# Attention scores in three float32r passes over high and low parts, and a new table of places for the attention steps

## The chip, the cores and the metric

The kernel runs on one core of one Trainium2 chip, in one launch. The metric is the device time in microseconds (us) of that launch. Engines are named as in the profile: PE is TensorE's matrix multiply, PEld its weight loads, DVE is VectorE, ACT is ScalarE, POOL is GpSimd, SP is SyncE, which here issues most DMAs.

## The reference

Three stages follow one another, all in float32:

```python
# 1. attention, batch 4, heads 8, sequence 576, head_dim 64
scores = q @ k.T / sqrt(64)
scores = where(scores >= max(scores) - tau, scores, -1e9)      # tau = 0.02
attn   = exp(scores - max(scores)); attn = attn / (sum(attn) + 1e-9)
out    = attn @ v                                              # -> x: 2304 rows of 512
# 2. mixture of experts, 8 experts, 512 -> 1024 -> 512, one expert per row
#    (argmax of the cosine of row and expert embedding)
# 3. the same again, the expert chosen by argmax(x @ w_gate)
```

The thresholding makes the scores' precision matter: which keys stay depends on differences of 0.02 and less.

## The kernel before, in words

**Attention** (class Attn, lines 127 to 500) takes the 32 heads as 16 pairs. For each pair: q and k of two heads are loaded by SP with the rows on the partitions (`load`); PE transposes them into a PSUM tile of the pool S (`transpose`, L226 to L231, steps `tk` and `tq`); ACT copies q out (L236, step `cpq`) and DVE copies k out (L237, step `cpk`). Then head A lies on partitions 0 to 63 and head B on 64 to 127 of the tiles Tq and Tk. The 576 queries of both heads make nine score tiles r of 128 queries x 576 keys (tile 8 holds the last 64 queries of both heads). Five steps `scores t` compute them (L240 to L249): for t < 4 the tiles 2t and 2t+1, one of each head, as matmuls of 64 rows by 288 keys that alternate between the heads, and for t = 4 tile 8 as matmuls of all 128 rows. All matmuls of attention are float32; the trace has two records, each with its own weight load, for one float32 matmul. So a step `scores t` is 8 records (t < 4) or 4 (t = 4).

Each score tile then goes `least` (DVE, L256: scaled copy out of PSUM and row minimum of the negated scores), `bound` (POOL, L263: threshold), and one of two ways to the unnormalised probabilities p. The first is `exp all` (ACT, L288), then `mask` (DVE, L293: compare with the threshold, multiply, row sum). The second is `beyond` (DVE, L268: a large number where the score is out), `add` (POOL, L272), `exp` (ACT, L283 with the row sum). `MASK_FIRST` (L137) lists the tiles that go the second way: 2, 4 and 6 in pairs 1 to 13, none in pair 0 and in the last two. After that PE transposes p in 128x128 blocks (L312, L310, steps `t A0` to `t R4`), ACT copies the blocks out (L322), PE multiplies by v (`av`, L338 and L334), ACT copies the result (L344), PE transposes it back and adds the router's logits (`out rows`, L354), DVE normalises (L362 to L367), SP stores. After every fourth pair the rows' places among the experts are worked out (`route`, on PE, DVE and POOL; `route slots` is 3.2 us of DVE in one step).

**The order** on each engine is fixed when the program is built. `ops` (L382 to L459) lists every step with its engine, an assumed duration, what it depends on and which buffers it takes and frees; `schedule` (L75) plays this list through, on each engine always the ready step with the lowest number `PERIOD * pair + PRIO[kind]`, and the steps are emitted in the order of their starts. `PERIOD` is 17.0 (L52) and `PRIO` a table by hand (L55 to L65). Buffers (L458): S, the PSUM tiles of transposed q, k and of scores, has two, so that a step `scores t` with t < 4 needs both; raw q and k, Tq and Tk two each, sn (scores out of PSUM) five, b three, p fourteen, raw v three.

**The expert layers** (class Moe) run afterwards; they already split every float32 operand into a high float32r part (ACT copy, L779) and a low one (DVE subtraction from PSUM, L782) and take three passes, high x high, high x low, low x high (L790, L801).

Of the kernel before, what the change touches and what calls it, by code (L numbers as in the profile page):

```python
# [22 lines left out]
B, H, S, D = 4, 8, 576, 64  # L23
# [25 lines left out]
BIG = 1e30  # L49
PAIRS = B * H // 2  # L50

PERIOD = 17.0  # L52


PRIO = {'first': -93.7, 'warm': -10000, 'emb norm': 10.0, 'emb t': 11.0, 'emb put': 12.0, 'params': 0.0, 'sign': 20.0, 'weights': 0.0,  # L55
        'ldk': -24.0, 'ldq': -24.0, 'ldv': -14.0, 'tk': -7.0, 'tq': -6.5, 'cpk': -6.5, 'cpq': -6.0,
        **{f'scores {t}': 3.2 * t for t in range(5)}, **{f'bound {t}': 3.2 * t + 2 for t in range(5)},
        **{f'least {r}': 1.6 * r + .5 for r in range(9)}, **{f'exp all {r}': 1.6 * r + 1.2 for r in range(9)}, **{f'mask {r}': 1.6 * r + 2 for r in range(9)},
        **{f'beyond {r}': 1.6 * r + 1 for r in range(9)}, **{f'add {r}': 1.6 * r + 1.5 for r in range(9)}, **{f'exp {r}': 1.6 * r + 3 for r in range(9)},
        'inverse': 17.0, **{f't {h}{k}': 16.0 + 2.6 * k + (h == 'B') for h in 'AB' for k in range(5)}, **{f'copy {h}{k}': 16.5 + 2.6 * k + (h == 'B') for h in 'AB' for k in range(5)},  # L60
        't R0': 29.5, 't R4': 30.0, 'copy R0': 30.0, 'copy R4': 30.5, **{f'av {k}': 18.0 + 2.6 * k for k in range(5)}, 'av R': 32.0,
        'out copy M': 30.0, 'out copy R': 32.5, 'out rows 0': 31.0, 'out rows 1': 32.0, 'out rows R': 33.0, 'out scale 0': 31.5, 'out scale 1': 32.5, 'out scale R': 33.5,
        'logits': 34.0, 'route argmax': 36.0, 'route prefix': 37.0, 'route count': 38.0, 'route slots': 38.0, 'route perm': 39.0, 'route add': 40.0,
        'plans': 20.0, 'choose count': 41.0, 'choose': 41.5,
        'w1 hi': 100.0, 'w1 lo': 101.0, 'ld w1': 102.0}  # L65


class Op:
# [4 lines left out]


def schedule(ops, caps, verbose=False):  # L75


# [49 lines left out]
class Attn:  # L127
# [6 lines left out]

    UNITS = [(h, k) for k in range(5) for h in 'AB'] + [('R', 0), ('R', 4)]

    MASK_FIRST = (), (2, 4, 6), ()  # L137
    DVE_COPY = (), (), ()

    def __init__(s, nc, tc, early, late, ident, q, k, v, tau, emb, xd, lg, moe):  # L140
# [89 lines left out]
        for t in range(4): nc.tensor.transpose(ps[:, 128 * t:128 * t + 128], raw[:, 128 * t:128 * t + 128], s.id)  # L230
        nc.tensor.transpose(ps[:, 512:512 + n], raw[0:n, 512:640], s.id[0:n, 0:n])  # L231

    def copy(s, j, nm):
        st = s.pair[j]
        st['T' + nm] = s.qk.tile([128, 640 if nm == 'q' else 576], F32, tag='T' + nm, name='T' + nm)
        if nm == 'q': s.nc.scalar.activation(out=st['Tq'], in_=st['psq'], func=AF.Copy)  # L236
        else: s.nc.vector.tensor_copy(st['Tk'], st['psk'])  # L237


    def scores(s, j, t):  # L240
        nc, st = s.nc, s.pair[j]
        q, k = st['Tq'], st['Tk']
        rr = (2 * t, 2 * t + 1) if t < 4 else (8,)
        for r in rr: st['ps', r] = s.psS.tile([128, 1024], F32, tag='S', name='psS')
        for i in range(2):
            ks = slice(i * 288, i * 288 + 288)
            for h, r in enumerate(rr):
                p = slice(64 * h, 64 * h + 64) if t < 4 else slice(0, 128)
                nc.tensor.matmul(st['ps', r][:, (224, 512)[i]:(512, 800)[i]], q[p, 128 * t:128 * t + 128], k[p, ks], start=True, stop=True)  # L249

    def least(s, j, r):

# [129 lines left out]
    def ops(s, params, done, prio=None):  # L382
# [13 lines left out]
        for j in range(PAIRS):  # L396
            ld, put = {}, {}
            for nm in 'kqv':
                if j == 0 and nm in 'kq': ld[nm] = op('ld' + nm, j, 'X', 0, lambda: None, alloc=['raw' + nm], lat=4.2 if nm == 'k' else 6.2)
                else: ld[nm] = op('ld' + nm, j, 'SP', 1.95 if nm == 'q' else 1.3, lambda j=j, nm=nm: s.load(j, nm), [first], alloc=['raw' + nm], lat=3.0)  # L400
            for nm in 'kq':
                step = lambda m, j=j, nm=nm: lambda: m(j, nm)
                x = op('t' + nm, j, 'P', .55, step(s.transpose), [ld[nm]], alloc=['S', 'T' + nm], free=['raw' + nm])
                if nm == 'k': put[nm] = op('cpk', j, 'D', .70, step(s.copy), [x], free=['S'])
                else: put[nm] = op('cpq', j, 'A', .60, step(s.copy), [x], free=['S'])
            if j == 0: emb.deps.append(put['k'])

            if j == 2:
                x = op('params', j, 'SP', 2.6, params, [last], lat=2.5)
                op('sign', j, 'D', .2, s.moe.sign, [x])  # L410
            if 1 <= j < 15: op('plans', j, 'G', 1.2, lambda j=j: s.moe.plans(j - 1), [last])

            P = {}
            for t in range(5):
                rr = (2 * t, 2 * t + 1) if t < 4 else (8,)
                last = op(f'scores {t}', j, 'P', 1.0, lambda j=j, t=t: s.scores(j, t), list(put.values()) + [last], t, alloc=['S'] * len(rr), free=[] if t < 4 else ['Tq', 'Tk'])
                least = [op(f'least {r}', j, 'D', .76, lambda j=j, r=r: s.least(j, r), [last], r, alloc=['sn'], free=['S']) for r in rr]
                th = op(f'bound {t}', j, 'G', .25, lambda j=j, t=t: s.bound(j, t), least, t)
                for r, l in zip(rr, least):
                    step = lambda m, r=r, j=j: lambda: m(j, r)  # L420
                    e = [emb_put] if j == 0 else []
                    if r not in s.of_pair(s.MASK_FIRST, j):
                        x = op(f'exp all {r}', j, 'A', .70, step(s.exp_all), [l], r, alloc=['b'])
                        P[r] = op(f'mask {r}', j, 'D', .80, step(s.mask), [x, th] + e, r, alloc=['P'], free=['sn', 'b'])
                    else:
                        x = op(f'beyond {r}', j, 'D', .50, step(s.beyond), [th], r, alloc=['b'])
                        x = op(f'add {r}', j, 'G', 1.36, step(s.add), [x], r, free=['sn'])
                        P[r] = op(f'exp {r}', j, 'A', .80, step(s.exp), [x] + e, r, alloc=['P'], free=['b'])
            inv = op('inverse', j, 'D', .5, lambda j=j: s.inverse(j), list(P.values()))

            U, AV, X = {}, None, []
            for u in s.UNITS:
                h, k = u
                n = f'{h}{k}'
                step = lambda m, a=u, j=j: lambda: m(j, a)
                rr = {'A': range(0, 8, 2), 'B': range(1, 8, 2), 'R': [8]}[h]
                small = u == ('R', 4)
                x = op('t ' + n, j, 'P', .11 if small else .44, step(s.unit_t), [P[r] for r in rr], alloc=['T'], free=['P'] * len(rr) if k == 4 else [])
                dve = u in s.of_pair(s.DVE_COPY, j)
                U[u] = op('copy ' + n, j, 'D' if dve else 'A', (.25 if small else .64) if dve else .2 if small else .5, step(s.unit_copy), [x], alloc=['r4' if small else 'u'], free=['T'])  # L440
                if h == 'A' or u == ('R', 0): continue
                big = h != 'R'
                kk = k if big else 'R'
                AV = op(f'av {kk}', j, 'P', .88 if big else .8, lambda j=j, kk=kk: s.unit_av(j, kk), ([AV] if big and AV else []) + [ld['v'], U['A' if big else 'R', k if big else 0], U[u]],
                        alloc=['A'] if k == 0 or not big else [], free=['u', 'u'] if big else ['u', 'r4'])
                if k < 4: continue
                hh = 'M' if big else 'R'
                x = op('out copy ' + hh, j, 'A', .5 if big else .2, lambda j=j, hh=hh: s.out_copy(j, hh), [AV], alloc=['avs' + hh], free=['A'])
                for a in (0, 1) if big else ('R',):
                    y = op(f'out rows {a}', j, 'P', .6 if big else .3, lambda j=j, a=a: s.out_rows(j, a), [x], alloc=['M'], free=['avs' + hh] if a else [])  # L450
                    X.append(op(f'out scale {a}', j, 'D', .37 if big else .4, lambda j=j, a=a: s.out_scale(j, a), [y, inv] + X[-1:], alloc=['xb'] if not a else [], free=['M']))
            op('v', j, 'X', 0, lambda: None, [AV, X[-1]], free=['rawv'])
            lg = op('logits', j, 'G' if j < PAIRS - 1 else 'D', .96 if j < PAIRS - 1 else .4, lambda j=j: s.logits(j), X, free=['xb'])
            if j % 4 == 3: counted = s.route(op, j, lg, counted)
            if j == 11: counted = s.choose(op, j, counted)
# [713 lines left out]
```

## Time and profile before

| what | value |
|---|---|
| median of 3 runs | 985.08 us (984.96 to 987.21) |
| the profiled execution, its own time | 985.7 us |
| its span, from first to last instruction | 984.0 us |
| mean granted TensorE clock | 0.957 of full speed |
| PE busy / DVE / ACT / POOL, share of the span | 93% / 62% / 50% / 34% |
| attention, about | the first 375 us |

The profile's span is cut in 40 slices of 24.6 us; attention fills the first fifteen. Shares of busy time over the whole span mix attention with the expert layers; the views by stretch separate them. Matmul records overlap (the end of one is modelled), so the time that an operation takes of PE is read from the distance of two starts, not from its duration.

### The profile page before, as it was taken

Reading aid. Unit: us, or ns where it says so; the run is one execution under the profiler, and the core shown is the slowest. Engines: PE = TensorE matmul, PEld = TensorE weight load, DVE = VectorE, ACT = ScalarE, POOL = GpSimd, SP = SyncE. Lnnn points to the kernel's source line nnn. Section 1 sums busy time; section 2 is a strip of 40 time slices with the busy share of each in tenths; the row PEclk is TensorE's granted clock in tenths of the full one; section 3 lists DMA queues with packets and bytes.
Section 4 is the critical chain, followed back from the end, with each engine's and each line's share of the span. In section 5 each row is a group of like instructions: output and inputs, shape, how many; then the busy total and the mean of one; then the engine's idle time right before and its main releaser. Section 6 shows DMA issues by size and latency. Waiting matters only on the chain. (4 is left out here: it accounts for less than half of the span.)

```text
span 984.0 us, 17399 instructions
## 1 busy us (share of the span) xinstructions
PE 914.2 (93%) x6174; PEld 765.2 (78%) x6174; DVE 613.0 (62%) x1487; ACT 495.7 (50%) x906; POOL 332.6 (34%) x610
## 2 busy tenths in 40 slices
PE   6999999999999995999999999986599999999993
PEld 4565655665665554999999999985599999999993
DVE  5777887888879855865744656654554253446540
ACT  3566666666765671745444556431254344545530
POOL 2143333323333121443443344433332241444230
PEclk7899999999999996999999999996699999999997
DMA  5222222222224202843444355233643254464500
GB/s 133 48 50 60 63 63 60 49 50 50 49 49 148 86 13 57 280 153 119 162 166 169 120 182 185 95 142 111 229 160 99 100 187 144 155 223 149 177 24 15
DMA packets 104080, 112.43 MB, mean 114 GB/s; under 512 B 68373, under 2 KB 73493, under 8 KB 103968
## 3 DMA queue, kind: packets, MB, share of 16 engines
q1 hardware_dynamic: 95968, 86.65, 29.0%
q0 software_dynamic: 8000, 24.43, 6.9%
q8 instruction: 53, 0.87, 0.4%
q14 instruction: 59, 0.48, 0.2%
HBM read 94.61 MB, written 18.53 MB: 115 GB/s over the span
## 5 line engine op out<-in xcount | busy, mean ns | idle before, releaser
L790 PE MATMUL l1p<-xh,w1h 128*128 128x256 f32 (+8 forms) x544 | 172.9, 318 | 7.6 <-SPq L1164 3.8
L790 PE MATMUL l1p<-xl,w1h 128*128 128x256 f32 (+8 forms) x544 | 168.9, 311 | 5.0 <-DVE xl L782 5.0
L801 PE MATMUL yps<-hh,w2h 128*128 128x256 f32 (+8 forms) x544 | 171.0, 314 | 0.0
L801 PE MATMUL yps<-hh,w2l 128*128 128x256 f32 (+8 forms) x544 | 167.6, 308 | 2.3 <-POOL w2l L723 2.3
L790 PE MATMUL l1p<-xh,w1l 128*128 128x256 f32 (+8 forms) x544 | 168.6, 310 | 0.0
L801 PE MATMUL yps<-hl,w2h 128*128 128x256 f32 (+8 forms) x544 | 167.3, 307 | 0.0
L322 ACT ACTIVATE u<-pt 128x512 f32<-128x512 f32 x192 | 105.2, 566 | 72.4 <-PE pt L312 68.7
L793 ACT ACTIVATE hh<-l1p 128x256 fp32r<-128x256 f32 (+8 forms) x136 | 58.9, 433 | 149.2 <-PE l1p L790 138.1
L256 DVE TENSOR_SCALAR_CACHE_REDUCE sn<-psS,nsc 128x576 f32<-128x576 f32 x144 | 113.7, 812 | 26.3 <-PE psS L249 25.6
L293 DVE SCALAR_TENSOR_TENSOR p<-sn,th,b 128x576 f32<-128x576 f32 x105 | 103.2, 994 | 19.7 <-ACT b L288 16.3
L249 PE MATMUL psS<-Tk,Tq 64*128 64x288 f32 (+1 forms) x576 | 108.9, 445 | 4.1 <-DVE sn L256 3.2
L795 DVE SCALAR_TENSOR_TENSOR hl<-l1p,hh 128x256 fp32r<-128x256 f32 (+8 forms) x136 | 64.6, 482 | 77.0 <-ACT hh L793 77.0
L790 PEld LDWEIGHTS l1p<-xh,w1h 128*128 128x128 f32 x544 | 104.8, 193 | 9.0 <-issue 4.1
L790 PEld LDWEIGHTS l1p<-xl,w1h 128*128 128x128 f32 x544 | 104.8, 193 | 5.5 <-DVE xl L782 5.3
L312 PEld LDWEIGHTS pt<-ident,p 128*128 128x128 f32 x640 | 69.7, 142 | 50.5 <-issue 40.8
L801 PEld LDWEIGHTS yps<-hh,w2l 128*128 128x128 f32 x544 | 102.6, 189 | 3.3 <-POOL w2l L723 2.9
L790 PEld LDWEIGHTS l1p<-xh,w1l 128*128 128x128 f32 x544 | 104.6, 192 | 0.2
L801 PEld LDWEIGHTS yps<-hl,w2h 128*128 128x128 f32 x544 | 102.8, 189 | 0.3
L801 PEld LDWEIGHTS yps<-hh,w2h 128*128 128x128 f32 x544 | 102.7, 189 | 0.4
L288 ACT ACTIVATE b<-sn,nm 128x576 f32<-128x576 f32 x105 | 80.6, 773 | 38.5 <-DVE sn L256 38.0
L312 PE MATMUL pt<-ident,p 128*128 128x128 f32 x640 | 94.7, 283 | 2.2 <-DVE p L293 1.1
L338 PE MATMUL av<-u,rawv 128*64 128x512 f32 x320 | 95.1, 616 | 1.2 <-ACT u L322 1.2
(211 smaller groups left out, 1448.9 us busy)
## 6 DMA issues: line engine op xcount, KB each, us to landing
rw<-in_moe_w_dram SPq DMA_DIRECT2D x128, 512.0 KB, 4.5
rawk<-in_k_dram SPq DMA_DIRECT2D x16, 256.0 KB, 3.4
rawq<-in_q_dram SPq DMA_DIRECT2D x16, 256.0 KB, 3.5
rawv<-in_v_dram SPq DMA_DIRECT2D x16, 256.0 KB, 3.1
xs<-xb SPq DMA_DIRECT2D x16, 256.0 KB, 3.1
rawk<-in_k_dram SPq DMA_DIRECT2D x16, 32.0 KB, 2.9
rawq<-in_q_dram SPq DMA_DIRECT2D x32, 16.0 KB, 2.8
rawv<-in_v_dram SPq DMA_DIRECT2D x16, 32.0 KB, 2.7
```

Source lines behind the costliest of these rows:

```text
L249: nc.tensor.matmul(st['ps', r][:, (224, 512)[i]:(512, 800)[i]], q[p, 128 * t:128 * t + 128], k[p, ks], start=True, stop=True)
L256: s.nc.vector.tensor_scalar(out=sn, in0=st.pop(('ps', r))[:, 224:800], scalar1=s.scale, scalar2=3e38, op0=ALU.mult, op1=ALU.min, accum_out ...
L288: s.nc.scalar.activation(out=b, in_=st['sn', r], func=AF.Exp, scale=-1.0, bias=s.of(st, 'nm', r))
L293: s.nc.vector.scalar_tensor_tensor(out=p, in0=st.pop(('sn', r)), scalar=s.of(st, 'th', r), in1=st.pop(('b', r)), op0=ALU.is_le, op1=ALU.mu ...
L312: for t in range(4): s.nc.tensor.transpose(pt[:, t * 128:t * 128 + 128], st['p', 2 * t + (h == 'B')][:, ks(k)], s.id)
L322: else: s.nc.scalar.activation(out=t, in_=pt, func=AF.Copy)
L338: nc.tensor.matmul(st['av'][64 * i:64 * i + 64], v(i, k), st.pop(('u', (h, k))), start=(k == 0), stop=(k == 4))
L790: s.nc.tensor.matmul(o, s.W1[a][k][:, fs], X[b][:, k, n0:n1], start=(q == 0), stop=(q == 3 * KC - 1))
L793: def hh(s, o, f, n0, n1): s.nc.scalar.activation(out=s.H[0][f][:, n0:n1], in_=o, func=AF.Relu)
L795: s.nc.vector.scalar_tensor_tensor(out=s.H[1][f][:, n0:n1], in0=o, scalar=0.0, in1=s.H[0][f][:, n0:n1].bitcast(F32), op0=ALU.max, op1=ALU. ...
L801: s.nc.tensor.matmul(ps, s.W2[a][f // 2][:, f % 2, ds], s.H[b][f][:, n0:n1], start=(f == 0 and q == 0), stop=(f == FC - 1 and q == 2))
```

## The change

Three parts. (1) Tq and Tk become two float32r tiles each: ACT writes the high part of both q and k (`high`), DVE subtracts it from the PSUM tile for the low part (`low`); the S buffer is freed only after `low`. A step `scores t` runs three float32r passes over each half of the keys. (2) In pairs 1 to 13 six tiles instead of three go by beyond, add and exp. (3) `PERIOD`, the whole table `PRIO` and some assumed durations are replaced.

```diff
-PERIOD = 17.0
+PERIOD = 18.42
-        'ldk': -24.0, 'ldq': -24.0, 'ldv': -14.0, 'tk': -7.0, 'tq': -6.5, 'cpk': -6.5, 'cpq': -6.0,
-        **{f'scores {t}': 3.2 * t for t in range(5)}, **{f'bound {t}': 3.2 * t + 2 for t in range(5)},
-        **{f'least {r}': 1.6 * r + .5 for r in range(9)}, **{f'exp all {r}': 1.6 * r + 1.2 for r in range(9)}, **{f'mask {r}': 1.6 * r + 2 for r in range(9)},
...
+PRIO = {... 'ldk': -55.3, 'ldq': -43.4, 'ldv': 16.7, 'tk': -27.6, 'tq': -59.2, 'hik': -33.7, 'hiq': 22, 'lok': -39.8, 'loq': 15.4, 'scores 0': -63.3,
+        'scores 1': -69.6, 'scores 2': -68.4, 'scores 3': -65.3, 'scores 4': -65.3, 'bound 0': -6.3, 'bound 1': -8, ...
+        'bound 3': -17.1, 'bound 4': -9, 'least 0': -17.3, ... 'exp all 0': -40, ... 'mask 0': -2.7, 'mask 1': 13, ...
+        'beyond 0': 12.9, ... 'add 0': 22.8, ... 'exp 0': 85.8, ... 't A0': 11, ... 'copy A0': 4.5, ... 'av 0': 21, ...
-    MASK_FIRST = (), (2, 4, 6), ()
+    MASK_FIRST = (), (1, 3, 4, 5, 7, 8), ()
-    def copy(s, j, nm):
+    def high(s, j, nm):
         st = s.pair[j]
-        st['T' + nm] = s.qk.tile([128, 640 if nm == 'q' else 576], F32, tag='T' + nm, name='T' + nm)
-        if nm == 'q': s.nc.scalar.activation(out=st['Tq'], in_=st['psq'], func=AF.Copy)
-        else: s.nc.vector.tensor_copy(st['Tk'], st['psk'])
+        st['T' + nm] = [s.qk.tile([128, 640 if nm == 'q' else 576], F32R, tag='T' + nm + p, name='T' + nm + p) for p in 'hl']
+        s.nc.scalar.activation(out=st['T' + nm][0], in_=st['ps' + nm], func=AF.Copy)
+    def low(s, j, nm):
+        st = s.pair[j]
+        s.nc.vector.tensor_tensor(out=st['T' + nm][1], in0=st.pop('ps' + nm), in1=st['T' + nm][0].bitcast(F32), op=ALU.subtract)
 ...
         for i in range(2):
             ks = slice(i * 288, i * 288 + 288)
-            for h, r in enumerate(rr):
-                p = slice(64 * h, 64 * h + 64) if t < 4 else slice(0, 128)
-                nc.tensor.matmul(st['ps', r][:, (224, 512)[i]:(512, 800)[i]], q[p, ...], k[p, ks], start=True, stop=True)
+            for n, (a, b) in enumerate(((0, 0), (0, 1), (1, 0))):
+                for h, r in enumerate(rr):
+                    p = slice(64 * h, 64 * h + 64) if t < 4 else slice(0, 128)
+                    nc.tensor.matmul(st['ps', r][:, (224, 512)[i]:(512, 800)[i]], q[a][p, ...], k[b][p, ks], start=(n == 0), stop=(n == 2))
 ...
-                if nm == 'k': put[nm] = op('cpk', j, 'D', .70, step(s.copy), [x], free=['S'])
-                else: put[nm] = op('cpq', j, 'A', .60, step(s.copy), [x], free=['S'])
+                x = op('hi' + nm, j, 'A', .70, step(s.high), [x])
+                put[nm] = op('lo' + nm, j, 'D', .76, step(s.low), [x], free=['S'])
 # assumed durations: scores 1.0 -> .95 (t < 4), .85 (t = 4); t (transposes of p) .44 -> .48, small .11 -> .12; av .88 -> 1.01
```

## Rows read from the trace of the kernel before

**Rows 1.** The page of the profiled execution: the 40 slices of PE and of the granted clock (tenths), and one row of the DMA issues (KB each, us from issue to landing).
```profile
PE   6999999999999995999999999986599999999993
...
PEclk7899999999999996999999999996699999999997
...
rawv<-in_v_dram SPq DMA_DIRECT2D x16, 256.0 KB, 3.1
```

**Rows 2.** PE by start time: the step `scores 4` (four records of 128 rows) of pairs 0, 2, 14 and 15, the first, third, fifteenth and last of sixteen such rows, and the operation right after that of pair 2. Columns: start us, us, engine, line, operation, tiles, shapes, records.
```profile
26.87 2.29 PE L249 MATMUL psS<-Tk,Tq 128*128 128x288 f32 x4 [0.33 <-DVE sn L256]
...
70.07 1.24 PE L249 MATMUL psS<-Tk,Tq 128*128 128x288 f32 x4
71.15 0.27 PE L310 MATMUL pt<-ident,p 128*128 128x128 f32 x1
...
333.09 1.24 PE L249 MATMUL psS<-Tk,Tq 128*128 128x288 f32 x4
...
352.33 1.14 PE L249 MATMUL psS<-Tk,Tq 128*128 128x288 f32 x4
```

**Rows 3.** Busy time by engine in the twelve pair periods between two of those rows (columns: stretch, its length, PE, PEld, DVE, ACT, POOL busy us with their counts, granted clock, DMA share, GB/s).
```profile
70.07:333.09 263.02, 257.03 (x1723) 156.68 (x1723) 217.92 (x560) 168.62 (x323) 89.38 (x321) 1.00 0.26 67
```

**Rows 4.** Waits of PE's weight loads in the same 263 us (what waited, for whom: us in total, times, longest); "issue" is time in which the profile shows no other engine to wait for.
```profile
PEld pt L312 <- issue: 31.8, 48, 0.8
PEld av L338 <- issue: 11.2, 42, 0.4
PEld psS L249 <- DVE sn L256: 9.2, 19, 0.8
...
PEld av L338 <- ACT u L322: 3.8, 10, 0.5
...
PEld pt L312 <- ACT u L322: 2.4, 5, 0.5
PEld pt L312 <- DVE p L293: 2.2, 5, 0.6
PEld xp L354 <- ACT avsM L344: 2.0, 4, 0.7
```

**Rows 5.** PE by start time in one stretch of pair 9: transposes of p, a step `scores t` with t < 4, transposes, an `av` step, the router's small matmuls.
```profile
208.00 1.09 PE L312 MATMUL pt<-ident,p 128*128 128x128 f32 x8
209.02 1.24 PE L249 MATMUL psS<-Tk,Tq 64*128 64x288 f32 x8
210.19 0.66 PE L312 MATMUL pt<-ident,p 128*128 128x128 f32 x4
210.78 1.08 PE L338 MATMUL av<-u,rawv 128*64 128x512 f32 x4
211.79 0.29 PE L620 MATMUL rp<-cnt,ones 128*128 128x40 f32 x1
211.92 0.59 PE L622 MATMUL rp<-roh,ones 128*128 128x32 f32 x4
212.37 0.27 PE L623 MATMUL rp<-roh,upr 128*128 128x40 f32 x1
```

**Rows 6.** PE by start time in the second expert layer, where one-pass float32r matmuls of the same 288 columns follow one another (the first two and the last of seventeen rows).
```profile
735.79 0.30 PE L790 MATMUL l1p<-xh,w1h 128*128 128x288 f32 x1
735.93 0.30 PE L790 MATMUL l1p<-xl,w1h 128*128 128x288 f32 x1
...
737.93 0.30 PE L790 MATMUL l1p<-xl,w1h 128*128 128x288 f32 x1
```

**Rows 7.** Matmuls and weight loads of L790 alone in a longer stretch there (columns: stretch, length, PE and PEld busy us with counts, clock, DMA share, GB/s).
```profile
731.20:745.40 14.20, 13.05 (x97) 12.92 (x98) 1.00 0.41 126
```

**Rows 8.** Groups of instructions between 50 and 350 us (busy us, mean ns of one, idle before and what ended it): the steps on DVE, POOL and ACT that the change touches.
```profile
L256 DVE TENSOR_SCALAR_CACHE_REDUCE sn<-psS,nsc 128x576 f32<-128x576 f32 x124 | 97.9, 811 | 19.0 <-PE psS L249 18.2
L293 DVE SCALAR_TENSOR_TENSOR p<-sn,th,b 128x576 f32<-128x576 f32 x88 | 88.7, 1017 | 15.2 <-ACT b L288 13.5 <-POOL th L263 0.9 <-issue 0.2
L268 DVE TENSOR_SCALAR b<-sn,th 128x576 f32<-128x576 f32 x37 | 21.4, 580 | 9.1 <-POOL th L263 9.0
L237 DVE COPY Tk<-psp 128x576 f32<-128x576 f32 x13 | 9.7, 749 | 0.0
L272 POOL TENSOR_TENSOR b<-sn,b 128x576 f32<-128x576 f32 x37 | 58.7, 1586 | 22.9 <-DVE b L268 13.7 <-ACT b L288 5.1 <-ACT u L322 3.2
L236 ACT ACTIVATE Tq<-psp 128x640 f32<-128x640 f32 x13 | 9.1, 701 | 0.7 <-PE psp L231 0.7
```

**Rows 9.** The same kind of step as the new `low`, in the expert layers: the low part subtracted out of PSUM (busy us, mean ns, idle before).
```profile
L782 DVE TENSOR_TENSOR xl<-xpt,xh 128x512 fp32r<-128x512 f32 x48 | 32.9, 689 | 45.1 <-ACT xh L779 45.0
```

**Rows 10.** DVE by start time: a mask beside a POOL add, a mask alone, a beyond alone and one beside a POOL step.
```profile
227.56 1.52 DVE L293 SCALAR_TENSOR_TENSOR p<-sn,th,b 128x576 f32<-128x576 f32 x1
...
230.04 0.80 DVE L293 SCALAR_TENSOR_TENSOR p<-sn,th,b 128x576 f32<-128x576 f32 x1
...
242.09 0.52 DVE L268 TENSOR_SCALAR b<-sn,th 128x576 f32<-128x576 f32 x1 [0.31 <-POOL th L263]
...
245.30 0.75 DVE L268 TENSOR_SCALAR b<-sn,th 128x576 f32<-128x576 f32 x1 [0.31 <-POOL th L263]
```

**Rows 11.** POOL by start time: the add beside that first mask, and an add during which DVE ran a mask.
```profile
227.05 1.41 POOL L272 TENSOR_TENSOR b<-sn,b 128x576 f32<-128x576 f32 x1 [0.46 <-DVE b L268]
...
242.76 2.02 POOL L272 TENSOR_TENSOR b<-sn,b 128x576 f32<-128x576 f32 x1 [0.70 <-ACT b L288]
```

More of the change, by code (lines that the diff above doesn't have):

```diff
@@ L50 @@
 PAIRS = B * H // 2
-PERIOD = 17.0
-PRIO = {'first': -93.7, 'warm': -10000, 'emb norm': 10.0, 'emb t': 11.0, 'emb put': 12.0, 'params': 0.0, 'sign': 20.0, 'weights': 0.0,
-        'ldk': -24.0, 'ldq': -24.0, 'ldv': -14.0, 'tk': -7.0, 'tq': -6.5, 'cpk': -6.5, 'cpq': -6.0,
-        **{f'scores {t}': 3.2 * t for t in range(5)}, **{f'bound {t}': 3.2 * t + 2 for t in range(5)},
-        **{f'least {r}': 1.6 * r + .5 for r in range(9)}, **{f'exp all {r}': 1.6 * r + 1.2 for r in range(9)}, **{f'mask {r}': 1.6 * r + 2 for r in range(9)},
[L59 to L65, printed above, removed]
@@ new lines @@
+PERIOD = 18.42
+PRIO = {'first': -93.7, 'warm': -10000, 'emb norm': 10, 'emb t': 11, 'emb put': 12, 'params': 0, 'sign': 20, 'weights': 0, 'ldk': -55.3,
+        'ldq': -43.4, 'ldv': 16.7, 'tk': -27.6, 'tq': -59.2, 'hik': -33.7, 'hiq': 22, 'lok': -39.8, 'loq': 15.4, 'scores 0': -63.3,
+        'scores 1': -69.6, 'scores 2': -68.4, 'scores 3': -65.3, 'scores 4': -65.3, 'bound 0': -6.3, 'bound 1': -8, 'bound 2': -11.3,
+        'bound 3': -17.1, 'bound 4': -9, 'least 0': -17.3, 'least 1': -16.9, 'least 2': -20.5, 'least 3': -16.6, 'least 4': -13, 'least 5': -7.2,
+        'least 6': -10.8, 'least 7': -1.5, 'least 8': -2.6, 'exp all 0': -40, 'exp all 1': -41.6, 'exp all 2': -47.8, 'exp all 3': -45.3,
+        'exp all 4': -42.4, 'exp all 5': -28.5, 'exp all 6': -49.8, 'exp all 7': -49.6, 'exp all 8': -38.7, 'mask 0': -2.7, 'mask 1': 13,
[3 rows of a table added]
+        'exp 1': 94.9, 'exp 2': 95.6, 'exp 3': 101.9, 'exp 4': 85.1, 'exp 5': 103.2, 'exp 6': 102.5, 'exp 7': 106.8, 'exp 8': 107.7, 'inverse': 88.2,
[4 rows of a table added]
+        'out scale 0': 46.2, 'out scale 1': 64.2, 'out scale R': 62.6, 'logits': 34, 'route argmax': 36, 'route prefix': 37, 'route count': 38,
+        'route slots': 38, 'route perm': 39, 'route add': 40, 'plans': 20, 'choose count': 41, 'choose': 41.5, 'w1 hi': 100, 'w1 lo': 101,
+        'ld w1': 102}
@@ L246, in scores @@
             ks = slice(i * 288, i * 288 + 288)
-            for h, r in enumerate(rr):
-                p = slice(64 * h, 64 * h + 64) if t < 4 else slice(0, 128)
-                nc.tensor.matmul(st['ps', r][:, (224, 512)[i]:(512, 800)[i]], q[p, 128 * t:128 * t + 128], k[p, ks], start=True, stop=True)
+            for n, (a, b) in enumerate(((0, 0), (0, 1), (1, 0))):
+                for h, r in enumerate(rr):
+                    p = slice(64 * h, 64 * h + 64) if t < 4 else slice(0, 128)
+                    nc.tensor.matmul(st['ps', r][:, (224, 512)[i]:(512, 800)[i]], q[a][p, 128 * t:128 * t + 128], k[b][p, ks], start=(n == 0), stop=(n == 2))
     def least(s, j, r):
@@ L415, in ops @@
                 rr = (2 * t, 2 * t + 1) if t < 4 else (8,)
-                last = op(f'scores {t}', j, 'P', 1.0, lambda j=j, t=t: s.scores(j, t), list(put.values()) + [last], t, alloc=['S'] * len(rr), free=[] if t < 4 else ['Tq', 'Tk'])
+                last = op(f'scores {t}', j, 'P', .95 if t < 4 else .85, lambda j=j, t=t: s.scores(j, t), list(put.values()) + [last], t, alloc=['S'] * len(rr), free=[] if t < 4 else ['Tq', 'Tk'])
                 least = [op(f'least {r}', j, 'D', .76, lambda j=j, r=r: s.least(j, r), [last], r, alloc=['sn'], free=['S']) for r in rr]
@@ L437, in ops @@
                 small = u == ('R', 4)
-                x = op('t ' + n, j, 'P', .11 if small else .44, step(s.unit_t), [P[r] for r in rr], alloc=['T'], free=['P'] * len(rr) if k == 4 else [])
+                x = op('t ' + n, j, 'P', .12 if small else .48, step(s.unit_t), [P[r] for r in rr], alloc=['T'], free=['P'] * len(rr) if k == 4 else [])
                 dve = u in s.of_pair(s.DVE_COPY, j)
@@ L443, in ops @@
                 kk = k if big else 'R'
-                AV = op(f'av {kk}', j, 'P', .88 if big else .8, lambda j=j, kk=kk: s.unit_av(j, kk), ([AV] if big and AV else []) + [ld['v'], U['A' if big else 'R', k if big else 0], U[u]],
+                AV = op(f'av {kk}', j, 'P', 1.01 if big else .8, lambda j=j, kk=kk: s.unit_av(j, kk), ([AV] if big and AV else []) + [ld['v'], U['A' if big else 'R', k if big else 0], U[u]],
                         alloc=['A'] if k == 0 or not big else [], free=['u', 'u'] if big else ['u', 'r4'])
```

7 rows, old and new, of the table PRIO are left out of this document.

## The prediction

> **What bounds the kernel now.** I read the page's slices first. In the fifteen slices that attention fills PE is busy for nine tenths or more in all but the first, and the granted clock is full from the third slice on [rows 1]. Attention is therefore PE's stage, and the expert layers after it are not edited. A busy PE need not be streaming, so I turn to starts. The step `scores 4` starts at 70.07 us in pair 2 and at 333.09 us in pair 14: 263.02 us for twelve pairs, 21.92 us a pair [rows 2]. From pair 0 (26.87) to pair 15 (352.33) it is 325.5 us for fifteen. In the twelve pairs PE is busy 257.0 us, DVE 217.9 (18.16 a pair), ACT 168.6 (14.05) and POOL 89.4 (7.45), at full clock [rows 3]. So PE is first, DVE second and not far behind. Last come the waits: PE's weight loads wait for another engine's result in many small pieces, of which the listed rows make 19.6 us [rows 4]. With the smaller ones I take 25 us, 2.1 us a pair: **places in the order where PE stands, though its records look dense**. The larger "issue" rows, never over 0.8 us each [rows 4], are left where they are: they fall at changes between kinds of step, and the change keeps the kinds.
>
> **The scores on PE.** A float32 step `scores t` with t < 4 takes 209.02 to 210.19, 1.17 us for eight records [rows 5]; a step `scores 4` takes 70.07 to 71.15, 1.08 us for four [rows 2]. Twice as many records of half the height cost nearly the same, so the two heads' matmuls run side by side: four slots in both. One slot is 288 columns twice over, by 2.4 GHz 0.24 us; four make 0.96, which leaves 0.21 and 0.12 us per step for starting and draining. Afterwards both kinds have six slots (two halves of the keys, three passes), each one pass of float32r. That price is in the expert layers: seventeen such matmuls of 288 columns start between 735.79 and 737.93, 2.14/16 = 0.134 us apart [rows 6]. Six slots are 0.80 us, so the steps become 1.01 and 0.92 us: **0.16 us off each of five steps, 0.80 us a pair**. Bounds: columns alone at 2.4 GHz give 0.12 a slot, another 0.08 off a step (1.2 us a pair in all); passes that do not run side by side are a rival below. The rows of before show no float32r pass on half the array; I take the 0.134 because the float32 halves did pair.
>
> **What is added elsewhere, a pair.** ACT: one more copy, `high` of k, at most the 0.70 us of q's [rows 8]. DVE loses k's copy (0.75) and three masks (1.02 each), and gains three beyonds (0.58 each) [rows 8] and two `low`. A low part of 512 columns takes 0.689 us [rows 9]; scaled by columns, an upper bound since a part is fixed, 0.78 for k and 0.86 for q. Sum: -0.75 - 3.05 + 1.74 + 1.64 = -0.42, so DVE goes from 18.16 to **17.7 us a pair**. POOL gains three adds of 1.59 [rows 8]: 7.45 to 12.2 of some 20. None of this lies on PE; what covers it is that PE needs more than each of them. If the cover goes, DVE is late next: at 17.7 it has about 2.5 us a pair to spare. The wait that is added is `low` behind `high`: a transposed tile holds its S buffer through an ACT copy and a DVE step, 0.7 + 0.8 us instead of one step of 0.7. PE's next scores queue behind that buffer, and behind them every transposition and av step emitted later. Bounds: nothing if PE is given transposes of p meanwhile, 0.8 us a pair for each tile if not. `bound` queues behind POOL's adds, and beyond and mask behind `bound`. I take nothing for these, because `tk`, `lok` and the scores are moved about three pairs ahead (numbers near -28 to -70 at 18.42 a pair), so a late tile has work to hide it (only q's copies stand late in line, at 22 and 15.4, on engines with time to spare), and put their upper ends into the rivals.
>
> **The places.** Everything in attention moves, SP's loads too: k and q go further ahead (-24 to -55.3 and -43.4) and wait for their two raw buffers, v goes back from -14 to 16.7, before the first av at 21. A v load lands 3.1 us after its issue [rows 1], and the 4.3 in between covers that narrowly; no load is added, so SP's queue is only reordered. The order before was laid out for 0.88 us an av step, of which the trace makes 210.78 to 211.79, 1.01 [rows 5], and 0.44 for four transposes, of which it makes 1.02/2 = 0.51 [rows 5]; the new order assumes 1.01 and 0.48. An order whose PE durations fit should stand less for others. Of the 2.1 us a pair between nothing and all may go (below nothing: a rival). I take 0.85, well under half: DVE's slack does not grow, and the route steps still fall into every fourth pair.
>
> **Start and tail.** Pair 0 gets one more step in its chain (`low` of q, 0.86 us) and shorter scores at the half clock, where `scores 4` shows 2.29 us for what takes 1.08 later [rows 2]. These cancel within a microsecond, and I put the start at nothing. After the last scores (352.33) PE works through pair 15's products as before.
>
> **Sum.** 0.80 + 0.85 = 1.65 us a pair, by the fifteen periods between the first and the last `scores 4`: 25 us. The profiled execution took 985.7 us (span 984.0 and 1.7 around it), 0.6 over the median of 985.1. 985.7 - 25 = 960.7; against the median 960.1. **I say 961 us.**
>
> **Rivals.** (a) *The places bring nothing*, because PE stood for buffers and for DVE and still does. For it: DVE's load stays. Then 0.80 x 15 = 12 us remain, about 973. If the S buffers' longer hold is exposed once a pair as well (0.8), that gain is used up too and the time is the same, 985.
> (b) *DVE and POOL block each other, and DVE becomes the bound*: the slower side. A mask takes 0.80 us alone and 1.52 beside an add [rows 10], a beyond 0.52 and 0.75 [rows 10], and the add 1.41 or 2.02 [rows 11]. With twice the adds, let all three masks take 1.52 instead of the mean 1.02 and six beyonds 0.75 instead of 0.58: +1.5 + 1.0, so DVE needs 20.2 us a pair. Today it idles 21.92 - 18.16 = 3.8. Where it keeps over 1.7 of these, a pair is longer than now; with 2.2 it is 22.4, and the time 985.7 + 15 x 0.5 = 993. Against it: three of the masks that collide are gone. The Trainium skill, page "SBUF — State Buffer", section "Who interferes with whom", has this as an exclusive lock, in which the second of the two waits for the whole of the first; the 1.52 beside 0.80 agrees.
> (c) *The passes do not overlap their weight loads*, or the halves do not pair. A load of 128 columns with hardly any matmul takes 0.45/4 = 0.11 us [rows 5]. Were it shown, a slot would be 0.11 + 0.134 = 0.244, six 1.46 and a step 1.67, 0.5 more than now: +2.5 - 0.85 us a pair, 985.7 + 25 = 1011. Against it: 97 loads and 97 matmuls of one shape filled 13.05 us [rows 7], 0.134 each, so the loads were hidden. The Trainium skill, page "TensorE: Matmul & The Clock Gate", section "The mechanism", says that a load overlaps a running matmul only where it goes to another group of rows, which speaks against this change; the 97 loads, all of full height, contradict it here.
> That the scores don't become cheaper though the passes are fewer is (c) in a milder form.
>
> **How the numbers follow.** The forecast's case (at least some of the standing goes, 943 to 967) has 0.62, (a) 0.22 at 968 to 982 and 0.05 unchanged, (b) 0.08, (c) 0.03. 943 is all of the standing and the cheapest slot, (2.1 + 1.2) x 15 = 50 under 985.7 would be 936, and few orders reach that. Faster: 0.62 + 0.22 = 0.84; within 0.3% (3 us, about what a measurement of this kernel can tell from no change) 0.05; slower 0.11. The range reaches from 943 to 982 and leaves out (b), (c) and the unchanged case, 0.16 together.
>
> **What would show it.** In the profile after: six starts of paired float32r matmuls about 0.13 us apart and a step of about 1.0 us; `scores 4` every 20.3 us in the middle; DVE's busy time near 17.7 us a pair; masks mostly near 0.8; the expert layers as long as before. A step of 1.2 us or more proves the scores' term wrong, a period of 21 us that of the places, and a DVE busy above 19 us a pair makes it (b).

## The result and the profile after

| | us |
|---|---|
| before, median of 4 runs | 985.06 (984.96 to 987.21) |
| changed, median of 4 runs | 952.05 (951.33 to 953.09) |
| ratio changed / before, 95% interval | 0.9661 (0.9644 to 0.9677) |
| forecast | 961, range 943 to 982 |
| profiled execution, its own time / span | 951.33 / 949.5 |

33 us came off, 25 had been forecast. The page of the changed kernel answers to [rows 1]: PE is just as dense, attention is shorter.

```profile
span 949.5 us, 18029 instructions
...
PE   6999999999999968999999999973999999999993
...
PEclk7899999999999988999999999985899999999997
```

PE by start time, the six one-pass records of `scores 4` in pairs 0, 2, 14 and 15 (the first record of each; of pair 15 the last too, with what follows), answering to [rows 2]:

```profile
27.05 0.61 PE L259 MATMUL psS<-Tkh,Tqh 128*128 128x288 f32 x1 [0.81 <-DVE sn L266]
...
67.58 0.40 PE L259 MATMUL psS<-Tkh,Tqh 128*128 128x288 f32 x1
...
304.50 0.40 PE L259 MATMUL psS<-Tkh,Tqh 128*128 128x288 f32 x1
...
320.96 0.40 PE L259 MATMUL psS<-Tkh,Tqh 128*128 128x288 f32 x1
...
321.73 0.30 PE L259 MATMUL psS<-Tkh,Tql 128*128 128x288 f32 x1
321.86 0.38 PE L320 MATMUL pt<-ident,p 128*128 128x128 f32 x2
```

From pair 0 to pair 15 it is 293.9 us where it was 325.5: 31.6 of the 34.5 us between the spans lie in these fifteen periods. In the twelve middle ones a pair takes 236.92/12 = 19.74 us, where it took 21.92. The start is as it was (27.05 against 26.87). Another 3.1 us lie behind the last scores, where the passage to the experts was run at a granted clock of 0.73 of full speed in its twenty us instead of 0.64.

Busy time by engine in those twelve periods (PE, PEld, DVE, ACT, POOL), answering to [rows 3]:

```profile
67.58:304.50 236.92, 236.92 (x1943) 159.08 (x1942) 199.38 (x535) 181.78 (x375) 137.12 (x355) 1.00 0.25 60
```

By its records, whose ends are modelled, PE has no idle time left; before it had 6 us. DVE is at 16.6 us a pair (18.16 before), ACT at 15.1, POOL at 11.4. Added up from start to start over these periods, the scores take 4.91 us of PE a pair (6.05 before), the transposes of p 5.85 (6.36), the av steps 5.94 (6.29) and `out rows` 1.28 (1.48). So half of the 2.2 us a pair is the scores' own; the rest lies in steps whose matmuls did not change.

Waits of PE's weight loads in the same window, answering to [rows 4]:

```profile
PEld pt L322 <- ACT u L332: 10.2, 22, 0.8
...
PEld psS L259 <- DVE sn L266: 5.7, 7, 0.8
PEld psp L236 <- DVE p L303: 4.9, 6, 0.8
```

All such rows behind DVE and ACT make 46.6 us, where they made 29.3 before, although PE idles less and the pair is shorter. The "issue" rows fell from 60.2 to 28.6 us. A weight load that waits is therefore not yet a PE that stands.

One step `scores t` and the av step after it, answering to [rows 5]:

```profile
161.97 0.49 PE L259 MATMUL psS<-Tkh,Tqh 64*128 64x288 f32 x2
162.21 0.39 PE L259 MATMUL psS<-Tkl,Tqh 64*128 64x288 f32 x2
162.34 0.39 PE L259 MATMUL psS<-Tkh,Tql 64*128 64x288 f32 x2
...
162.74 0.38 PE L259 MATMUL psS<-Tkh,Tql 64*128 64x288 f32 x2
163.05 1.08 PE L348 MATMUL av<-u,rawv 128*64 128x512 f32 x4
```

Two records start within 0.1 us of each other in each slot, and after the first, slots follow 0.13 us apart. This step takes 161.97 to 163.05, 1.08 us; `scores 4` above takes 320.96 to 321.86, 0.90 us. The scores' 4.91 us a pair leave 1.0 for the mean step with t < 4.

DVE and POOL in the middle of attention (67 to 320 us; busy, mean ns of one, idle before), answering to [rows 8]:

```profile
L303 DVE SCALAR_TENSOR_TENSOR p<-sn,th,b 128x576 f32<-128x576 f32 x48 | 38.5, 809 | 4.4 <-ACT b L298 3.5 <-POOL th L273 0.5
L278 DVE TENSOR_SCALAR b<-sn,th 128x576 f32<-128x576 f32 x68 | 38.2, 589 | 0.1
L246 DVE TENSOR_TENSOR Tql<-psp,Tqh 128x640 fp32r<-128x640 f32 x12 | 9.8, 813 | 0.1
...
L246 DVE TENSOR_TENSOR Tkl<-psp,Tkh 128x576 fp32r<-128x576 f32 x12 | 9.0, 748 | 0.3 <-ACT Tkh L242 0.3
...
L282 POOL TENSOR_TENSOR b<-sn,b 128x576 f32<-128x576 f32 x69 | 102.0, 1491 | 42.2 <-DVE b L278 31.3 <-ACT u L332 9.2 <-ACT p L293 1.4
```

A mask takes 0.81 us where it took 1.02, although POOL adds twice as often. An add takes 1.49 (1.59 before), a beyond the same 0.59.

### The profile page after: what moved, and what is told of

It is laid out like the page before. It is cut to its first block, busy times and chain, and to the rows that moved or that the text cites. A ratio compares the mean times of both kernels' runs of the same rounds, so it can differ in the third digit from the quotient of the medians.

```text
span 949.5 us, 18029 instructions
## 1 busy us (share of the span) xinstructions
PE 885.5 (93%) x6462; PEld 768.9 (81%) x6462; DVE 594.6 (63%) x1464; ACT 509.0 (54%) x961; POOL 387.4 (41%) x649
## 5 line engine op out<-in xcount | busy, mean ns | idle before, releaser
L282 POOL TENSOR_TENSOR b<-sn,b 128x576 f32<-128x576 f32 x78 | 114.9, 1486 | 51.3 <-DVE b L278 38.9
L332 ACT ACTIVATE u<-pt 128x512 f32<-128x512 f32 x192 | 102.6, 567 | 34.7 <-PE pt L322 23.4
L322 PEld LDWEIGHTS pt<-ident,p 128*128 128x128 f32 x640 | 69.8, 142 | 34.4 <-ACT u L332 16.3
L348 PE MATMUL av<-u,rawv 128*64 128x512 f32 x320 | 88.8, 616 | 0.0
L741 POOL DMA_INDIRECT out_dram<-y,idx x26 | 26.6, 1023 | 146.5 <-ACT y L824 48.6
L733 DVE TENSOR_TENSOR w2l<-rw,w2h 128x1024 fp32r<-128x1024 f32 x48 | 63.0, 1325 | 33.9 <-ACT w2h L732 33.9
```

The source lines that it names most:

```text
L282: s.nc.gpsimd.tensor_tensor(out=st['b', r], in0=st.pop(('sn', r)), in1=st['b', r], op=ALU.add)
L322: for t in range(4): s.nc.tensor.transpose(pt[:, t * 128:t * 128 + 128], st['p', 2 * t + (h == 'B')][:, ks(k)], s.id)
L332: else: s.nc.scalar.activation(out=t, in_=pt, func=AF.Copy)
L348: nc.tensor.matmul(st['av'][64 * i:64 * i + 64], v(i, k), st.pop(('u', (h, k))), start=(k == 0), stop=(k == 4))
L733: def split_lo(s, W, R, k, eng): eng.tensor_tensor(out=W[1][k], in0=R[k], in1=W[0][k].bitcast(F32), op=ALU.subtract)
L741: if s.last: s.nc.gpsimd.indirect_dma_start(out=s.dst, out_offset=off, in_=y[:, 0:DM], in_offset=None, bounds_check=N - 1, oob_is_err=False)
```

## The experiments

The experiments first took the three parts apart. The planner plays the step list anew in every kernel whose list, numbers or durations differ, so the order differs there too; e2, e3, e6 and e13 keep the changed kernel's order exactly, and e12 that of e4. All times are medians of four runs, nine for e7; ratios are against runs of the kernel before on the same chip (985.8 to 986.9 there).

| places | tiles by beyond | float32 scores | three passes |
|---|---|---|---|
| old | three | 985 (before) | e1: 997.0, ratio 1.0103 (1.0086 to 1.0120) |
| old | six | e9: 977.8, 0.9919 (0.9898 to 0.9940) | e11: 965.5, 0.9797 (0.9780 to 0.9814) |
| new | three | e12: 975.4, 0.9892 (0.9873 to 0.9910) | e4: 961.0, 0.9750 (0.9733 to 0.9766) |
| new | six | e2: 966.3, 0.9802 (0.9786 to 0.9818) | 952.05 (changed) |

**e1, the passes alone.**

```diff
 # of the changed kernel; high, low and the three passes stay
-PERIOD = 18.42, PRIO, durations as changed
+PERIOD = 17.0, PRIO as before with 'hik': -6.5, 'lok': -6.5, 'hiq': -6.0, 'loq': -6.0, durations as before
-    MASK_FIRST = (), (1, 3, 4, 5, 7, 8), ()
+    MASK_FIRST = (), (2, 4, 6), ()
```

> The three float32r passes with high and low parts, but the table of places, the period, the assumed durations and the three tiles by beyond and add as before. Theory (passes worth 0.8 us a pair on PE, places worth the rest): 0.80 x 15 = 12 us off, 973 us; scores step 1.0 us, period of scores 4 about 21.1 us. Rival 1 (the passes bring nearly all, the places little): 955 to 960. Rival 2 (the S buffer that is held through high and low is exposed, PE stands longer): 983 to 990.

Measured 997.0: 11 us slower than before. My theory fell; the second rival had the direction, and the loss is larger than its range. Busy times and waits in its twelve periods (73.26 to 346.44 us):

```profile
73.26:346.44 273.18, 253.42 (x1941) 165.02 (x1940) 222.10 (x568) 175.78 (x335) 92.67 (x321) 0.99 0.25 64
```

```profile
PEld psS L253 <- DVE sn L260: 13.0, 17, 1.9
...
PEld pt L316 <- ACT u L326: 7.4, 12, 1.2
...
PE psS L253 <- DVE sn L260: 4.7, 8, 1.7
```

The last of these rows is of PE itself; before, in the window of [rows 3], it was

```profile
PE psS L249 <- DVE sn L256: 1.3, 3, 0.7
```

A pair takes 22.77 us. PE idles 19.8 us of the 273: 7.4 ahead of transposes of p, 5.9 ahead of scores, 4.9 ahead of `out rows`. It stands for `least`, which frees the S buffers, longer than before. DVE is at 18.5 us a pair and itself idle for a fifth of the time. No engine is full. The loop through two S buffers is one place where PE stands, and not the largest.

**e2, the changed kernel's order with float32 scores.**

```diff
+   Tq, Tk 'h' tiles F32 instead of F32R (high copies the full values; low stays)
-            for n, (a, b) in enumerate(((0, 0), (0, 1), (1, 0))):
+            # one float32 matmul per head and half, q[0], k[0], start=True, stop=True
```

> The changed kernel with the scores in float32 as before (one float32 matmul per head and half, from the high tile, which then holds the full values; low is still computed, as a subtraction that gives zero and is not used); order, high and low steps unchanged. Theory (PE is the only bound of attention in the new order): each of five steps costs 0.16 us more, 0.83 a pair with the measured steps, 15 x 0.83 = 12 us over 952: 964.5. Rival (the passes matter more than their own length, since a longer step makes the following ones late): 970 or more. Rival (DVE or buffers bound the new order, PE has slack): under 957.

Measured 966.3, 14.2 us over the changed kernel. Its twelve periods take 20.58 us each, 0.84 more; I had forecast 0.80 and expected 0.83 here. The theory holds: in this order PE is the bound, and the passes are worth their own length. From start to start the scores take 5.76 us a pair here and 4.91 in the changed kernel, and every other kind of step on PE takes the same in both, within 0.03.

**e3, one head after the other.**

```diff
-            for n, (a, b) in enumerate(((0, 0), (0, 1), (1, 0))):
-                for h, r in enumerate(rr):
+            for h, r in enumerate(rr):
+                for n, (a, b) in enumerate(((0, 0), (0, 1), (1, 0))):
```

> The changed kernel with all three passes of one head before those of the other, per half of the keys; the same matmuls in another order. Theory (two matmuls run side by side only when neighbours in the order go to different halves of the rows): only one of the five neighbours in six is of the other half, so a step takes about 10 to 12 slots of 0.134 plus 0.2, 1.5 to 1.8 us instead of 1.0, +2.0 to 3.2 us a pair: 982 to 1000. Rival (PE reorders enough to pair them anyway, as it may have done with the two records of a float32 matmul): 952 to 955.

Measured 954.4, ratio 0.9675 (0.9652 to 0.9698), the changed kernel's within the intervals. The rival held. The same step in its trace:

```profile
161.19 0.48 PE L259 MATMUL psS<-Tkh,Tqh 64*128 64x288 f32 x2
161.43 0.38 PE L259 MATMUL psS<-Tkl,Tqh 64*128 64x288 f32 x2
161.56 0.37 PE L259 MATMUL psS<-Tkh,Tql 64*128 64x288 f32 x2
...
161.96 0.37 PE L259 MATMUL psS<-Tkh,Tql 64*128 64x288 f32 x2
162.25 1.08 PE L348 MATMUL av<-u,rawv 128*64 128x512 f32 x4
```

The program has high x high, low x high, high x low of one head and then those of the other. The starts show both heads' high x high first, at 161.19 and 161.27: the second head's first matmul starts ahead of the first head's second one (161.43), which stands two places before it in the kernel's text. That nothing puts them in another order on the way to PE's queue is taken for granted; the trace tells starts alone.

**e4, three tiles by beyond in the new places.**

```diff
-    MASK_FIRST = (), (1, 3, 4, 5, 7, 8), ()
+    MASK_FIRST = (), (3, 5, 8), ()
```

> The changed kernel with three tiles (3, 5, 8) by beyond, add and exp in the middle pairs, where the change has six. Theory (PE bound, DVE has 3 us a pair to spare in the new order): DVE gains three masks of 0.75 to 1.0 and loses three beyonds of 0.45, +0.9 to 1.7 us of 16.6 a pair, all beside PE: 952 to 956. Rival (the six tiles are what took DVE off PE's path): 962 to 975.

Measured 961.0, 9 us over the changed kernel, on the edge of the rival. A pair takes 20.38 us and DVE is at 17.3 of them (67.39 to 311.92 us):

```profile
67.39:311.92 244.53, 239.96 (x1946) 159.88 (x1942) 207.12 (x572) 175.75 (x337) 87.09 (x321) 1.00 0.29 72
```

Three more masks a pair, on an engine with three us of slack, cost 9 us. PE's own waits in these periods:

```profile
PE pt L322 <- ACT u L332: 2.3, 5, 0.9
PE psp L236 <- DVE sn L266: 0.8, 2, 0.4
PE xp L364 <- DVE xb L377: 0.7, 1, 0.7
```

PE never stands ahead of the scores, and they take 4.91 us a pair, as in the changed kernel. Longer are the transposes of p (6.27 us a pair against 5.85) and `out rows` (1.45 against 1.28). So the nine us are not lost where the scores wait for their S buffers, and the transposes of q and k, which need one too, wait 0.8 us in all twelve. Whether the nine come from DVE's time or from the other order of the steps is not told apart.

**e5, the passes with the old table and the new durations.**

```diff
 # of e1
-   scores 1.0, transposes .44, av .88
+   scores .95 / .85, transposes .48, av 1.01
```

> As e1 (passes with the old table, period and three tiles by beyond), but with the changed kernel's assumed durations (scores .95 and .85, four transposes .48, av 1.01). e1 took 997 us, 11 more than before. Theory A (the order is bad because the planner's durations are wrong): most of the loss goes, 970 to 980. Theory B (the hand-written places are what makes PE stand, whatever durations the planner assumes): 990 to 1000.

Measured 993.9, ratio 1.0083 (1.0061 to 1.0105): theory B. True durations alone do not repair the table by hand.

**e7, the S buffer freed after high.**

```diff
 # of e1
-    out=st['T' + nm][1], in0=st.pop('ps' + nm), in1=st['T' + nm][0].bitcast(F32), op=ALU.subtract
+    out=st['T' + nm][1], in0=st['T' + nm][0].bitcast(F32), in1=st['T' + nm][0].bitcast(F32), op=ALU.subtract
 # high takes st.pop('ps' + nm); free=['S'] moves from the step low to the step high
```

> As e1, but the S buffer is free again after high: low subtracts the high tile from itself in SBUF (so the low parts are zero, and the scores carry the high parts alone); the number and kind of steps on PE, ACT and DVE stay. Theory (the passes lose time in the old places because a transposed tile holds its S buffer 2 us longer for q, 0.4 for k): the 12 us of shorter scores come through, 970 to 980. Rival (the loss is the added DVE and ACT work, 1.5 us a pair on DVE): 990 to 1000.

Measured 984.3 in all; the scores differ here, so attention is compared. `scores 4` of pair 15 in e1 and in e7:

```profile
363.41 0.40 PE L253 MATMUL psS<-Tkh,Tqh 128*128 128x288 f32 x1
```

```profile
350.26 0.40 PE L253 MATMUL psS<-Tkh,Tqh 128*128 128x288 f32 x1
```

13 us come back with the buffer, of the 24 by which e1 missed its 973. The theory holds for that half. The other half stays (352.33 before [rows 2] less 12 would be 340). Since the planner plays the list anew with the buffer free earlier, the hold itself and the order that it forces are not told apart. In its twelve periods PE idles 12.7 us where it idled 19.8, but ahead of the scores only 3.7 instead of 5.9: most of what came back is not ahead of them.

**e9, six tiles by beyond alone.**

```diff
 # of the kernel before
-    MASK_FIRST = (), (2, 4, 6), ()
+    MASK_FIRST = (), (1, 3, 4, 5, 7, 8), ()
```

> The kernel before with one edit: six tiles (1, 3, 4, 5, 7, 8) go by beyond, add and exp in the middle pairs instead of three; float32 scores, old table. Theory (with the old places PE stands for the order, and the extra POOL adds make p later): 985 to 1000. Rival (relief of DVE is worth the 9 us here too that three against six tiles made in the new places): 973 to 980.

Measured 977.8, 8 us off (ratio 0.9919): the rival. Twelve periods of its trace:

```profile
67.07:324.82 257.75, 252.12 (x1732) 156.88 (x1731) 189.63 (x524) 171.07 (x362) 135.32 (x355) 1.00 0.27 68
```

A pair takes 21.48 us instead of 21.92 with DVE at 15.8 instead of 18.16. The part that I had priced at nothing is worth 8 us with nothing else edited; the order, played anew, changed with it. Of the 8, the twelve periods hold 5.3. PE idles there about as long as before (5.6 us against 6.0): less ahead of the scores (0.2 against 1.4), more ahead of transposes of p (4.4 against 2.1).

**e11, passes and six tiles in the old places.** Edit: e1 with `MASK_FIRST` of six tiles.

> Passes and six tiles by beyond, both with the old table of places and the old durations (e1 and e9 together). Theory (parts add up: +11 for the passes in the old places, -8 for the six tiles): 988. Rival (the passes lost in e1 because DVE was late to free the S buffers; with the DVE time of three masks gone they give their 12 us): 966 to 972.

Measured 965.5 (ratio 0.9797): the rival's number. With six tiles the passes give 12.3 us in the old places (977.8 to 965.5; 10.6 between the spans of the two profiled executions), about the twelve forecast; with three tiles they had cost 11. The rival's reason holds in part: from e1 to here PE's idle time in twelve periods falls from 19.8 to 2.4 us, ahead of the scores from 5.9 to nothing, ahead of transposes of p from 7.4 to 1.5, ahead of `out rows` from 4.9 to 0.1.

```profile
68.57:314.45 245.88, 243.47 (x1945) 162.94 (x1944) 195.78 (x538) 177.36 (x373) 136.61 (x356) 1.00 0.28 72
```

20.49 us a pair, PE idle 2.4 us in all; DVE 16.3 a pair. The new places take this from 965.5 to 952.05: 13.5 us.

**e12, the places alone.** Edit: e2 with `MASK_FIRST` of the tiles 3, 5 and 8.

> The new table, period and durations with float32 scores (as e2) and three tiles by beyond (3, 5, 8, as e4): the places alone. Theory (the passes are worth 14 us in the new places, as between e2 and the changed kernel, whatever the tiles): 961 + 14 = 975. Rival (float32 scores cover the DVE time of three tiles, so that the third part is worth nothing without the passes): 966.

Measured 975.4 (ratio 0.9892): the theory. "Alone" is not quite so: this kernel and e2 keep `high` and `low` with the longer hold of S, and the three tiles are 3, 5 and 8 instead of 2, 4 and 6. In the new places the columns of the table differ only in the scores' matmuls, in the old ones also in `high`, `low` and the hold. In the new places the passes are worth 14 us with three tiles (975.4 to 961.0) and with six (966.3 to 952.05), and six tiles 9 us with either kind of scores.

**e10, the new table with the old durations.**

```diff
 # of the changed kernel
-   scores .95 / .85, transposes .48, av 1.01
+   scores 1.0, transposes .44, av .88
```

> The changed kernel with the old assumed durations (scores 1.0, transposes .44, av .88), the table and the period as changed. Theory (the table of numbers makes the order, the durations little): 950 to 958. Rival (numbers and durations fit each other alone): 965 or more.

Measured 974.1, ratio 0.9885 (0.9865 to 0.9904): the rival. The numbers of the table are worth nothing under other durations: 22 us are lost, more than the places bring. Of these at most some 5 are the clock's (granted 0.98 over its twelve periods of 255.49 us, 1.00 in the changed kernel). PE idles 10.7 us there, 7.7 of them ahead of `out rows`, where it waits for DVE's normalising:

```profile
PE xp L364 <- DVE xb L377: 7.6, 6, 2.3
```

**e13, the S buffer freed after high in the changed order.** Edit: the subtraction of e7 in the changed kernel, the planner's list untouched.

> The changed kernel in its own order, only that low subtracts the high tile from itself in SBUF, so that a transposed tile's S buffer is free after high (low parts are zero, which changes the scores and can change the experts' share of rows; so attention alone is compared). Theory (in the new order PE never stands for that buffer): scores 4 of pair 15 starts at 320 to 322 us as in the changed kernel, 19.7 us a pair. Rival (the hold of S still costs PE): 310 or less, 19.0 a pair.

Neither: `scores 4` of pair 15 starts later, at 329.28 us, 20.57 us a pair (959.2 us in all). The edit had a second effect, which spoils it as a test of the hold. POOL and DVE of e13, by start time:

```profile
170.00 3.58 POOL L282 TENSOR_TENSOR b<-sn,b 128x576 f32<-128x576 f32 x2 [0.47 <-DVE b L278]
170.27 2.03 DVE L246 TENSOR_TENSOR Tql<-Tqh 128x640 fp32r<-128x640 f32 x1
...
172.22 1.98 DVE L246 TENSOR_TENSOR Tkl<-Tkh 128x576 fp32r<-128x576 f32 x1
```

and the same two steps in the changed kernel, DVE first, then POOL:

```profile
186.79 0.81 DVE L246 TENSOR_TENSOR Tql<-psp,Tqh 128x640 fp32r<-128x640 f32 x1
187.86 0.76 DVE L246 TENSOR_TENSOR Tkl<-psp,Tkh 128x576 fp32r<-128x576 f32 x1 [0.26 <-ACT Tkh L242]
```

```profile
186.53 2.98 POOL L282 TENSOR_TENSOR b<-sn,b 128x576 f32<-128x576 f32 x2
```

With one operand in PSUM, `low` takes 0.81 and 0.76 us in the middle of two adds; with both in SBUF it takes 2.03 and 1.98 beside the same adds. That is 2.4 us a pair more on DVE, and the period grew by 0.83: rival (b)'s mechanism, in a kernel made for something else. That it is the add beside them, and not SBUF alone, is shown by e7, where the same step with both operands in SBUF falls beside no add:

```profile
L240 DVE TENSOR_TENSOR Tql<-Tqh 128x640 fp32r<-128x640 f32 x11 | 9.1, 823 | 1.1 <-ACT Tqh L236 1.1
```

**e6, two passes.**

```diff
-            for n, (a, b) in enumerate(((0, 0), (0, 1), (1, 0))):
+            for n, (a, b) in enumerate(((0, 0), (0, 1))):     # stop=(n == 1)
```

> The changed kernel without the third pass (low part of q times high part of k), which leaves that part of the scores out. Theory (PE is still the bound, 0.134 us for each of ten slots a pair): 1.3 us a pair, 15 x 1.3 = 20 us off 952: 932. Rival (DVE, 16.6 us of 19.74 a pair, or the S buffers take over): 938 to 952.

Measured 937.5 in all; in attention 18.78 us a pair, 0.96 less, where ten slots of 0.134 would be 1.3. Three quarters arrive, at the rival's edge, though PE still hardly idles (64.39 to 289.77 us). From start to start the scores themselves go from 4.91 to 3.87 us a pair, so most of the missing part is in the slots, 0.104 us each instead of 0.134:

```profile
64.39:289.77 225.38, 223.41 (x1727) 143.78 (x1725) 198.77 (x534) 180.46 (x374) 137.06 (x355) 1.00 0.26 62
```

DVE is at 198.77/12 = 16.6 of 18.8 us there.

## Why the prediction was right, and where it was not

**The scores on PE: right.** Slots are 0.13 us, `scores 4` takes 0.90 (0.92 forecast), and e2 against the changed kernel, in one order, gives 0.84 us a pair where 0.80 had been taken. The float32 steps as read off beforehand, 4 x 1.17 + 1.08, are the 5.76 us that the scores take in e2; of the 6.05 that they took before, the remaining 0.29 belong to the order. Rival (c) is out: the pairs run side by side, with a weight load for every one-pass record.

**The places: the size was right, by luck, and the reason is open.** 0.85 us a pair, 13 us, had been taken; e11 to the changed kernel is 13.5, before to e12 9.7 (with the added steps in it). But the 2.1 us a pair of which I took a part were waits of weight loads, and these grew, from 29.3 to 46.6 us behind DVE and ACT in twelve periods; PE itself idled only 6.0 us, half a microsecond a pair. The "issue" rows, which I had left where they are since the kinds of step stay, are what fell (60.2 to 28.6 us). Nor is it shown that the places work because the planner's durations fit: e5, the new durations with the old numbers, brings 3 us, and e10 shows only that the new numbers go with the durations for which they were made. Why the same transposes and av steps take less of PE in the new order stays open.

**What is added elsewhere: this step failed.** "None of this lies on PE" was read from busy shares, and so the third part got no price. It is worth 8 us alone (e9) and 9 in the new places (e4). Busy time was the wrong measure; how the part reaches PE is known only for some of the kernels. `least` is DVE's, and it frees the two S buffers on which PE's scores wait: in the old places with the passes, the six tiles take PE's standing ahead of the scores from 5.9 us to nothing in twelve periods (e1, e11), though more goes elsewhere. In the new places this is not the way: with three tiles or six, PE never stands ahead of the scores, and the time goes at transposes of p and `out rows` (e4). That it is DVE's relief that pays, and not the order that the planner makes of another list, was not tested. DVE's sum was off as well: it came to 16.6 us a pair, not 17.7, mostly because masks take 0.81 instead of 1.02. In the fifteen periods 31.6 us came off where 25 had been forecast, so about 7 are missing there, the size of this part; the 3.1 us behind the last scores stood in no term.

**The added wait (low behind high): its price was real, its cover was another.** I had let it cost nothing, since scores are placed further ahead, and had put its upper end into "unchanged, 985". In the old places with three tiles it costs more than the passes bring (e1: 997), and e7 gives 13 us of that back. My case (a), "973 if the places bring nothing", does not exist in that form: without the places the result is 997 or, with the six tiles, 965.5. Either the new places or the six tiles cover the wait. What makes up the rest of e1's loss is open; DVE's 0.3 us a pair more is a candidate that was not tried. The granted clock is at half (1.2 GHz) for 3.4 us of its twelve periods, after PE had stood, which can be worth 1.7 us at most.

**Rival (b): its mechanism was right, its place was not.** Collisions fell: masks went from 1.02 to 0.81 us beside twice the adds. Adds now fall mostly beside steps that read PSUM. Added up from starts and ends in the trace, DVE works beside an add for 7.6 us a pair, of which `least` 4.1, `low` 1.6 and masks 0.2; before it was 4.2 us, of which masks 2.5. A `least` takes 0.81 us beside an add as well as alone, while before a mask took 0.81 alone and 1.31 (mean of 35) beside one. I had let every mask and beyond collide; nothing in [rows 10] said how often two such steps meet in another order.

**The sum.** Taken in one order through the table: six tiles 985 to 977.8, passes to 965.5, places to 952.05, that is 7, 12 and 13.5. The forecast was 0, 12 and 13. In another order the shares differ: passes first cost 11 (e1), and the six tiles then bring 31. Forecast period 20.3 us, measured 19.74.

## What to carry to other kernels

Work on an engine with slack is not free: three masks a pair on a DVE that was 83% busy were worth 8 to 9 us, and busy shares could not show it. To see how long PE stands and where its time goes, add up its own starts; waits of weight loads grew here while PE stood less. A cheaper step that holds a buffer longer can lose alone and win in company, so parts of a change need to be run in combinations before one is called useless. Beside POOL's adds, place DVE steps that take an operand from PSUM.

## What the runs showed of the hardware

PE ran matmuls on the two halves of its rows out of program order: in e3 the second head's first matmul started before the first head's second, and a step of twelve took no longer than with the heads in alternation (1.06 us against 1.08). The Trainium skill, page "TensorE: Matmul & The Clock Gate", section "The mechanism", says that matmuls start and end strictly in program order; for starts on different halves of the rows this trace shows otherwise.

A DVE step with two SBUF operands took 2.03 us beside POOL adds (e13), 0.82 beside none (e7), and 0.81 beside adds with one of them in PSUM (changed kernel), for the same 640 columns. The Trainium skill, page "SBUF — State Buffer", section "Who interferes with whom", says that a DVE instruction with two SBUF inputs contends with a GpSimd instruction that reads SBUF, and these rows agree with it.

One SBUF operand is not always safe: a `beyond`, which reads `sn` and a column of thresholds, took 1.67 us in the changed kernel beside an add, where others take 0.52 alone.

```profile
80.13 1.67 DVE L278 TENSOR_SCALAR b<-sn,th 128x576 f32<-128x576 f32 x1
```

```profile
79.44 2.04 POOL L282 TENSOR_TENSOR b<-sn,b 128x576 f32<-128x576 f32 x1
```
